# Third group's k and v loads ahead of its block loads on the SP queue, and two of five second-level factor sets made one group later

## The chip, the cores and the metric

The kernel runs on one core of one Trainium2 chip. The metric is the device time of one execution in microseconds (us), as the median of several runs. The kernel before takes 689.92 us (three runs, 687.94 to 690.47); its profiled execution has a span of 691.5 us, and all times inside the kernel below are counted from the start of that span.

## The reference

Decayed linear attention by blocks, followed by a two-layer network with the activation h − tanh(h). There are 4 batches, 8 heads, 768 positions and a head dimension of 64; the network maps 512 to 2048 to 512 for 3072 tokens, all in float32.

```python
for b in range(nb):                                  # blocks of 64 positions
    intra = (qb @ kb^T * Dmask) @ vb                 # within the block, with powers of lam
    inter = (qb * lam_pow) @ kv_state                # from all blocks before
    out[:, :, sl] = intra + inter
    kv_state = lam_block * kv_state + (kb * rev_pow)^T @ vb
x = out.transpose(0, 2, 1, 3).reshape(3072, 512)
h = x @ w_in
out = (h - tanh(h)) @ w_out
```

## The kernel before, in words

**Groups.** The kernel works in blocks of 128 positions instead of 64. There are six groups, numbered 0 to 5: group g is positions 128g to 128g+127 of all four batches, which is 512 tokens. A pair (g, b) of a group and a batch is a chunk. A group passes through attention (`att_transpose`, `att_scores`, `att_out`, `att_state`, in two halves of two batches), then the first layer (`up`), then the second layer (`down`, `down_twice`). Attention of group g+1 is interleaved with the network of group g.

**Plain and split products.** Group 0 uses ordinary matrix products (`up_plain`, `down_plain`). Its second layer is also where the 64-bit weights are turned into 32-bit ones, and where `sums_out` forms the sums of blocks of w_out and writes them to memory. From group 1 on, each layer is split into quarters and done with seven products instead of eight (Strassen's scheme in Winograd's form), called P1 to P7. In the second layer, five of the seven (P3 to P7, the list `TWICE`) are split a second time: `down_twice` has seven small products of 128 columns, 56 matmuls in all, where `down` has 32 matmuls of 256 columns. `down_twice` needs sums of quarters of the hidden values (`sums_twice`, `low`) and has corrections on DVE after the products. The second split needs a factor set of w_out in memory for each product (`fine`).

**Making the factor sets.** For P4, P5, P6, P7 and P3 (`MADE`, numbered t = 0 to 4), `load_quarters(t)` (L452) fetches four quarters of 256 KB from `factors`, into the ring of weight pieces (tag "wb", for even t) or of output tiles (tag "o", four buffers, for odd t). `factors_twice(t)` (L463) does four subtractions on DVE (L468) and four stores of 256 KB to `fine` (L470). All five are spread over the first layer of group 1, after its 6th, 11th, 15th, 20th and 24th product (`turns`).

**Pieces.** The second layer's weights come in pieces of 256 KB through a ring of seven buffers (`piece`, L472), from `fine` (L479) or `factors` (L482). They are issued on the GpSimd queue (POOL in the profile), together with the quarters, the stores to `fine` and the output stores (`store`, L490). The order is written down in `stream`.

**Loads of attention.** They run on the queue of SyncE (SP in the profile). Groups 0 and 1 load q, k and v as they lie ("natural", L127), and TensorE transposes q and k. From group 2 on (`GB` = 2), q and k also come as blocks of 32 by 32 (`load_blocks`, L140, 16 transfers of 16 KB for one chunk's q or k), which DVE transposes (L283). They go into a pool of seven buffers for the eight tiles of a group. This pool takes memory that staging for the weights used before, so its first load has to wait for the last weights to be finished (L260). k in natural form has three buffers, v has four; DVE multiplies k by the decay in place (L318), and TensorE uses k and v in `att_state` (L323) and v in `att_out` (L354). `load` (L143) fixes the order on the queue for a whole group:

```python
for b in range(B - 1):
    load_blocks(g, b, "qk")
load_blocks(g, 3, "q")
for b in (0, 1):
    load_natural(g, b, nat)
load_blocks(g, 3, "k")
for b in (2, 3):
    load_natural(g, b, nat)
```

**Order around the change.** In the last loop, each group runs its first layer (`up` for u = 0 to 3, with P1 of the next u ahead), with the first half of attention of the next group in it; then P1, P2, P4, P5, P6, P7 and P3 of the second layer, with the rest of attention between them. P1 of the next group's first layer runs between P7 and P3. Every engine does its own instructions in the order in which they were compiled, which is close to the order of the program but not the same.

Of the kernel before, what the change touches and what calls it, by code (L numbers as in the profile page):

```python
# [14 lines left out]
AL = mybir.AluOpType  # L15

BLK = 128
GB = 2
# [5 lines left out]
def kernel(  # L24
# [31 lines left out]
    nc = tc.nc  # L56
# [6 lines left out]
    NG = S // BLK  # L63
    HB = GRP // 2
    NU = DFF // 512
# [56 lines left out]
    def load_natural(g, b, names):  # L122
        for name, src, bufs in (("q", q, 2), ("v", v, 4), ("k", k, 3)) if (g, b) == (0, B - 1) else (
                ("q", q, 2), ("k", k, 3), ("v", v, 4)):
            if name in names:
                x = (qpool if name == "q" else io).tile([128, H, D], F32, name=f"{name}_nat", tag=name, bufs=bufs)
                op = nc.sync.dma_start(out=x, in_=src[b, :, ts(g, BLK), :].rearrange("h s d -> s h d"))  # L127
                if g >= GB:
                    tc.keep_in_program_order(op)
                raw[g, b][name] = x  # L130
# [12 lines left out]
    def load(n):  # L143

        while at["loaded"] < min(n, len(chunks)):
            g, b = chunks[at["loaded"]]
            if g < GB:
                raw[g, b] = {}  # L150
                load_natural(g, b, "qkv")
                at["loaded"] += 1
                continue
            for b in range(B):
                raw[g, b] = {}
            nat = "kv" if g < NG - 1 else "v"
            for b in range(B - 1):
                load_blocks(g, b, "qk")
            load_blocks(g, 3, "q")
            for b in (0, 1):  # L160
                load_natural(g, b, nat)
            load_blocks(g, 3, "k")
            for b in (2, 3):
                load_natural(g, b, nat)
            at["loaded"] += B


# [8 lines left out]
    TWICE = (3, 5, 6, 4, 7)  # L176
# [84 lines left out]


    load(B)
    load_weights(WAHEAD)

# [3 lines left out]
    def bank(name, tag, bufs):  # L269
        return psum.tile([128, 512], F32, name=name, tag=tag, bufs=bufs)  # L270
# [110 lines left out]
    def product_bank(key, n):  # L381

        if n == 1:
            banks[key, "y"] = bank("y", "yb" if key[0] == "up" and key[2] % 2 else "ya", 1)
        if n in (2, 5):
            banks[key, "zw"[n == 2]] = bank("zw"[n == 2], "zw"[n == 2], 1)
        t = banks[key, {2: "w", 5: "z", 3: "z"}.get(n, "y")]
        return t.rearrange("q (m c) -> q m c", m=2), n in (1, 2, 5)
# [51 lines left out]
    RING = 7  # L440

    def twice(g, n):
        return n in TWICE and not (g == NG - 1 and n == 3)

    stream = [(g, n, x) for g in range(1, NG) for n in (1, 2, 4, 5, 6, 7, 3)
              for x in (SUB if twice(g, n) else range(NU))]
# [2 lines left out]
    MADE = (4, 5, 6, 7, 3)  # L449
    quarters = {}  # L450

    def load_quarters(t):  # L452
        src = factors[XAT[FACT[MADE[t]][1]]].rearrange("p (u m) c -> p u m c", m=2)
        for i in range(2):
            for j in range(2):
                if t % 2 == 0:
                    x = late["pool"].tile([128, NU, 128], F32, name="wq", tag="wb", bufs=RING)
                else:
                    x = opool.tile([128, NU, 128], F32, name="oq", tag="o")
                nc.gpsimd.dma_start(out=x, in_=src[:, :, i, ts(j, 128)])  # L460
                quarters[t, i, j] = x
# [25 lines left out]
    def store(g, c, t):  # L487
        i, j = divmod(c - 11, 10)
        rows = out.rearrange("(b s) d -> s b d", b=B)[ts(g, BLK), 2 * i:2 * i + 2, ts(j, 256)]
        nc.gpsimd.dma_start(out=rows, in_=t.rearrange("q (m c) -> q m c", m=2))  # L490

    def otile(name):
        return opool.tile([128, 512], F32, name=name, tag="o")

    res, low = {}, {}
# [5 lines left out]

    def down(g, n):

        t, first = product_bank(("down", g), n)
        a = hidden(g, HIDAT[FACT[n][0]])
        for u in range(NU):
            wb = piece(g, n, u)
            for m in range(2):
                for kt in range(2):
                    nc.tensor.matmul(out=t[:, m, :], lhsT=a[:, u, kt, ts(m, 128)], rhs=wb[:, kt, :],  # L510
                                     start=first and u == 0 and m == 0 and kt == 0, stop=u == NU - 1 and kt == 1,
                                     skip_group_check=True)
        t = t.rearrange("q m c -> q (m c)")
        if n == 1:
            res[g, 1] = otile("q1")
            nc.scalar.activation(res[g, 1], t, AF.Copy)
        else:
            o11 = late["pool"].tile([128, 512], F32, name="o11", tag="o11", bufs=1)
            nc.vector.tensor_tensor(o11, res[g, 1], t, op=AL.add)
            store(g, 11, o11)  # L520
            sums_once(g, 11, "S1", 11)
# [6 lines left out]
    def sums_twice(g, n):  # L528
        a11, a12, a21, a22 = quarter(g, n)
        s1, s2 = (late["pool"].tile([128, NU, 128], F32, name=f"s{x}", tag="sums", bufs=4) for x in (1, 2))  # L530
        nc.vector.tensor_tensor(s1, a21, a22, op=AL.add)
        nc.vector.tensor_tensor(s2, s1, a11, op=AL.subtract)
        nc.vector.tensor_tensor(a21, a11, a21, op=AL.subtract)
        low[g, n] = (s1, s2)
# [79 lines left out]
    def run(pieces):  # L614
        for fn, *args in pieces:
            fn(*args)
# [32 lines left out]
    late["blk"] = ctx.enter_context(tc.tile_pool(name="blk", bufs=2 * B - 1))  # L649
    late["pool"] = ctx.enter_context(tc.tile_pool(name="late", bufs=1))  # L650

    turns, made = (6, 11, 15, 20, 24), []
    load_quarters(0)
    load_quarters(1)
    up(1, 0, 1)
    for g in range(1, NG):
        last = g == NG - 1
        p0, p1 = attention(g + 1) if not last else ([], [])
        for u in range(NU):
            for n in (2, 6, 5, 7, 1, 4, 3):  # L660
                if n != 1:
                    up(g, u, n)
                elif u + 1 < NU:
                    up(g, u + 1, 1)
                else:
                    down(g, 1)
                if g == 1:
                    made.append(n)
                    if len(made) in turns:
                        t = turns.index(len(made))  # L670
                        factors_twice(t)
                        if t + 2 < len(MADE):
                            load_quarters(t + 2)
            if not last and u > 1:
                run(p0[u - 2:u - 1])
        sums_twice(g, 4)
        down(g, 2)
        run(p0[2:])
        sums_twice(g, 5)
        down_twice(g, 4, "z")  # L680
        run(p1[0:1])
        sums_once(g, 21, 21, 11)
        sums_twice(g, 6)
        down_twice(g, 5, "w")
        run(p1[1:2])
        sums_twice(g, 7)
        down_twice(g, 6, "z")
        if not last:
            sums_twice(g, 3)
        run(p1[2:])  # L690
        down_twice(g, 7, "w")
        if not last:
            up(g + 1, 0, 1)
            down_twice(g, 3, "z")
        else:
            down_end(g)

# [29 lines left out]
```

## Time and profile before

| what | value |
|---|---|
| median of three runs | 689.92 us |
| span of the profiled execution | 691.5 us |
| transfers | 123.27 MB, 178 GB/s on average |
| second layer and attention beside it, group 1 | 203.17 to 278.70 us |
| the same of group 2 | 322.03 to 384.77 us |
| the same of group 3 | 428.00 to 491.63 us |
| DVE's L468, one | 0.69 us |
| a load of k or v, 256 KB, issue to landing | 5.0 and 5.1 us |
| a piece from `fine`, 256 KB, issue to landing | 4.0 us |
| a piece from `factors`, 256 KB, issue to landing | 5.4 us |

PE is TensorE's matmul, PEld its loading of weights, DVE is VectorE, ACT is ScalarE. The profile gives the busy time of each engine, a picture of the span in 40 slices of 17.29 us with the busy share in tenths and TensorE's granted clock (PEclk, in tenths of full speed), the waits (who waited for whom, total, times, longest), the timeline of an engine (start, length, line, operation, and in brackets the idle time before it with what ended it), and windows (for each stretch its length, then busy time and number of instructions by engine, granted clock, the busy share of the DMA engines, GB/s). Names such as `wb<-fine` are destination and source.

### The profile page before, as it was taken

The numbers are of one execution on the slowest core, as the hardware profiler recorded it, in microseconds if no ns is written. First come the engines' busy times: TensorE is split into PE (matmuls) and PEld (weight loads), VectorE is DVE, ScalarE is ACT, GpSimd is POOL, SyncE is SP. The second block draws the span as 40 slices with busy tenths as digits, with TensorE's granted clock in tenths as the row PEclk, the third lists the DMA queues.
The fourth block names the chain that finished last, engine by engine and source line by source line (L and its number), as shares of the span: only waits on it lengthen the run. The fifth ranks groups of instructions, "written<-read, shape, count | busy, mean of one in ns | idle before, by whom it ended". The sixth has DMA issues, their size and how long they took to land.

```text
span 691.5 us, 12449 instructions
## 1 busy us (share of the span) xinstructions
PE 669.2 (97%) x4688; PEld 578.2 (84%) x4688; DVE 449.9 (65%) x786; ACT 194.5 (28%) x392; POOL 188.0 (27%) x325
## 2 busy tenths in 40 slices
PE   6799999999999689999999999999999999999998
PEld 5588855558887689888899988899988899988897
DVE  3697858893897576447787357787356786344653
ACT  2655432423321112232112233122233122233120
POOL 0001334217554144100144200144300254300262
PEclk9999999999999799999999999999999999999999
DMA  9869889739988798533498632598720576600385
GB/s 190 199 196 238 252 244 262 259 88 264 287 263 242 163 274 246 147 64 67 127 282 247 176 62 47 142 259 227 226 48 18 130 221 206 203 1 0 104 285 176
DMA packets 160427, 123.27 MB, mean 178 GB/s; under 512 B 133488, under 2 KB 133872, under 8 KB 160368
## 3 DMA queue, kind: packets, MB, share of 16 engines
q0 software_dynamic: 27504, 91.77, 41.8%
q1 hardware_dynamic: 132720, 30.71, 22.8%
q8 instruction: 37, 0.61, 0.4%
q14 instruction: 22, 0.18, 0.1%
q10 hardware_dynamic: 144, 0.00, 0.0%
HBM read 99.62 MB, written 22.81 MB: 177 GB/s over the span
## 4 chain that ended last, share of the span: by engine, by line
PE 79%; DMA 9%; issue 4%; SPq 4%; DVE 3%; POOL 1%; ACT 0%; DVEq 0%; POOLq 0%
PE y L405 16%; PE y L548 11%; PE z L405 8%; PE h L590 8%; PE zw L548 8%; PE w L510 5%; PE op L606 5%; PE y L510 4%; PE w L405 4%; SPq L140 3%; PE sp L303 3%; DMA k_blk<-in_k_dram 3%; DMA wb<-fine 3%; PE op L354 2%; DMA q_blk<-in_q_dram 2%
## 5 line engine op out<-in xcount | busy, mean ns | idle before, releaser
L479 POOL DMA_DIRECT2D wb<-fine x168 | 90.3, 538 | 144.0 <-PE y L548 56.8
L482 POOL DMA_DIRECT2D wb<-factors x44 | 23.9, 545 | 188.9 <-PE y L510 177.2
L405 PE MATMUL y<-xt,w 128*128 128x256 f32 x320 | 73.2, 379 | 0.0
L405 PEld LDWEIGHTS y<-xt,w 128*128 128x128 f32 x320 | 60.5, 190 | 8.5 <-issue 0.5
L413 ACT ACTIVATE th<-g 128x512 f32<-128x512 f32 x60 | 37.8, 630 | 93.8 <-DVE g L431 41.8
L548 PE MATMUL y<-wb,g 128*128 128x128 f32 x456 | 61.6, 279 | 0.0
L551 ACT ACTIVATE q<-y 128x128 f32<-128x128 f32 x96 | 26.7, 278 | 123.3 <-PE y L548 119.7
L414 DVE TENSOR_TENSOR g<-g,th 128x512 f32<-128x512 f32 x60 | 41.4, 690 | 27.5 <-ACT th L413 27.2
L548 PEld LDWEIGHTS y<-wb,g 128*128 128x128 f32 x456 | 56.0, 193 | 1.5 <-issue 0.3
L590 PE MATMUL h<-xt,w 128*128 128x256 f32 x256 | 56.8, 384 | 0.0
L606 PE MATMUL op<-wt,g 128*128 128x512 f32 x128 | 56.5, 595 | 0.0
L590 PEld LDWEIGHTS h<-xt,w 128*128 128x128 f32 x256 | 48.9, 192 | 7.4 <-issue 0.5
L606 PEld LDWEIGHTS op<-wt,g 128*128 128x128 f32 x128 | 23.8, 190 | 27.7 <-issue 26.5
L426 DVE TENSOR_TENSOR g<-g,z 128x512 f32<-128x512 f32 x20 | 13.7, 686 | 44.4 <-ACT g L425 44.4
L548 PE MATMUL zw<-wb,g 128*128 128x128 f32 x304 | 40.2, 275 | 0.0
L405 PE MATMUL y<-tt,w 128*128 128x256 f32 x160 | 37.9, 380 | 0.6 <-ACT g L425 0.6
L405 PE MATMUL z<-tt,ws 128*128 128x256 f32 x160 | 37.9, 380 | 0.0
L405 PE MATMUL w<-xt,w 128*128 128x256 f32 x160 | 37.8, 379 | 0.0
L405 PE MATMUL y<-tt,ws 128*128 128x256 f32 x160 | 37.8, 379 | 0.0
L405 PE MATMUL z<-xt,ws 128*128 128x256 f32 x160 | 37.8, 379 | 0.0
L307 DVE TENSOR_TENSOR ss<-sp,mask 128x512 f32<-128x512 f32 x48 | 30.8, 684 | 10.3 <-PE sp L303 10.3
L548 PEld LDWEIGHTS zw<-wb,g 128*128 128x128 f32 x304 | 37.0, 192 | 0.0
(125 smaller groups left out, 1223.7 us busy)
## 6 DMA issues: line engine op xcount, KB each, us to landing
wb<-fine POOLq DMA_DIRECT2D x168, 256.0 KB, 4.0
wb<-factors POOLq DMA_DIRECT2D x44, 256.0 KB, 5.4
raw<-in_moe_w_out_dram POOLq DMA_DIRECT2D x16, 512.0 KB, 5.4
v_nat<-in_v_dram SPq DMA_DIRECT2D x24, 256.0 KB, 5.1
factors<-wt POOLq DMA_DIRECT2D x8, 768.0 KB, 5.4
k_nat<-in_k_dram SPq DMA_DIRECT2D x20, 256.0 KB, 5.0
raw<-in_moe_w_in_dram SPq DMA_DIRECT2D x8, 512.0 KB, 5.4
raw<-in_moe_w_in_dram SPq DMA_DIRECT2D x16, 256.0 KB, 4.8
```

The costliest lines, as they stand in the source:

```text
L140: nc.sync.dma_start(out=x[ts(c, 32), p], in_=blk.rearrange("(r t) a -> t r a", t=32)))
L307: nc.vector.tensor_tensor(ss[:, j], sp[j], mask[:, j], op=AL.mult)
L405: nc.tensor.matmul(out=t[:, m, :], lhsT=wt[:, kt, ts(m, 128)], rhs=x[:, kt, :], start=first and m == 0 and kt == 0, stop=kt == 1, skip_gro ...
L413: nc.scalar.activation(th, src, AF.Tanh)
L414: nc.vector.tensor_tensor(dst(c), src, th, op=AL.subtract)
L479: nc.gpsimd.dma_start(out=t.rearrange("p m c -> p (m c)"), in_=fine[TWICE.index(n_), SUB.index(x_)].rearrange("p u c -> p (u c)"))
L482: nc.gpsimd.dma_start(out=t, in_=factors[XAT[FACT[n_][1]]][:, 2 * x_:2 * x_ + 2, :])
L510: nc.tensor.matmul(out=t[:, m, :], lhsT=a[:, u, kt, ts(m, 128)], rhs=wb[:, kt, :], start=first and u == 0 and m == 0 and kt == 0, stop=u = ...
L548: nc.tensor.matmul(out=dst, lhsT=a[:, u, :], rhs=wb[:, ts(u, 128)], start=x in (1, 2) and u == 0, stop=u == NU - 1, skip_group_check=True)
L551: nc.scalar.activation(keep, dst, AF.Copy)
L590: nc.tensor.matmul(out=hm[:, m, :], lhsT=w1[u][:, i, a, ts(m, 128)], rhs=xt[0, t][:, i, :], start=m == 0 and i == 0, stop=i == KI - 1, ski ...
L606: nc.tensor.matmul(out=obank[b], lhsT=g, rhs=wt[:, 2 * a:2 * a + 2, :], start=kt == 0 and a == 0, stop=kt == KH - 1 and a == 1)
```

## The change

For group 2 alone (`g == GB`), k and v of the chunks 0, 1 and 2 are loaded ahead of all block loads; the k and v of chunk 3 stay behind them. Of the five factor sets, only those of P4, P5 and P6 are made in the first layer of group 1, after its 7th, 14th and 21st product; those of P7 and P3 are made in the first layer of group 2, after its 8th and 18th. Their quarters use output tiles. In group 1, P7 and P3 are therefore done as plain products by `down`, with their output additions read straight from PSUM; from group 2 on they are split twice as before. The purpose is to have k and v there when attention of the third group asks for them, and to take loads, stores and sums out of the busiest stretch.

```diff
             nat = "kv" if g < NG - 1 else "v"
+            first = (0, 1, 2) if g == GB else ()
+            for b in first:
+                load_natural(g, b, nat)
             for b in range(B - 1):
                 load_blocks(g, b, "qk")
             load_blocks(g, 3, "q")
             for b in (0, 1):
-                load_natural(g, b, nat)
+                if b not in first:
+                    load_natural(g, b, nat)
             load_blocks(g, 3, "k")
             for b in (2, 3):
-                load_natural(g, b, nat)
+                if b not in first:
+                    load_natural(g, b, nat)
...
-        return n in TWICE and not (g == NG - 1 and n == 3)
+        return n in TWICE and not (g == NG - 1 and n == 3) and not (g == 1 and n in (7, 3))
...
-                if t % 2 == 0:
+                if t in (0, 2):
                     x = late["pool"].tile([128, NU, 128], F32, name="wq", tag="wb", bufs=RING)
                 else:
                     x = opool.tile([128, NU, 128], F32, name="oq", tag="o")
...
-        t, first = product_bank(("down", g), n)
+        if n in (1, 2):
+            t, first = product_bank(("down", g), n)
+        else:
+            t, first = bank("plain", "w" if n == 7 else "z", 1).rearrange("q (m c) -> q m c", m=2), True
...
+        elif n == 7:
+            o = otile("q7")
+            nc.vector.tensor_tensor(res[g, 4], res[g, 4], t, op=AL.add)
+            store(g, 21, res[g, 4])
+            nc.vector.tensor_tensor(o, res[g, 5], t, op=AL.add)
+            store(g, 22, o)
+        elif n == 3:
+            o = otile("q3")
+            nc.vector.tensor_tensor(o, res[g, 5], t, op=AL.add)
+            store(g, 12, o)
...
-    turns, made = (6, 11, 15, 20, 24), []
+    turns, made = {1: (7, 14, 21), 2: (8, 18)}, []
...
-                if g == 1:
+                if g in turns:
                     made.append(n)
-                    if len(made) in turns:
-                        t = turns.index(len(made))
+                    step = len(made) - 7 * NU * (g - 1)
+                    if step in turns[g]:
+                        t = turns[g].index(step) + len(turns[1]) * (g - 1)
                         factors_twice(t)
-                        if t + 2 < len(MADE):
-                            load_quarters(t + 2)
+                        if t in (0, 3):
+                            load_quarters({0: 2, 3: 4}[t])
+                    elif (g, step) == (2, 1):
+                        load_quarters(3)
...
-        sums_twice(g, 7)
+        if twice(g, 7):
+            sums_twice(g, 7)
         down_twice(g, 6, "z")
-        if not last:
+        if twice(g, 3):
             sums_twice(g, 3)
         run(p1[2:])
-        down_twice(g, 7, "w")
+        if twice(g, 7):
+            down_twice(g, 7, "w")
+        else:
+            down(g, 7)
         if not last:
             up(g + 1, 0, 1)
-            down_twice(g, 3, "z")
+            if twice(g, 3):
+                down_twice(g, 3, "z")
+            else:
+                down(g, 3)
```

## The prediction

> **What bounds the kernel now.** I read the page first: engine shares, then the tenths by slice. PE is busy for 97% of the span, so time can only come from PE's few gaps or from its instruction count.
>
> ```profile
> PE 669.2 (97%) x4688; PEld 578.2 (84%) x4688; DVE 449.9 (65%) x786; ACT 194.5 (28%) x392; POOL 188.0 (27%) x325
> ...
> PE   6799999999999689999999999999999999999998
> ...
> PEclk9999999999999799999999999999999999999999
> ```
>
> The two dips in PE (its slices 13 and 14, counted from 0, are 224.7 to 259.3 us) and the dip in the granted clock fall together. Next the waits of PE over the whole span: which wait ends last there.
>
> ```profile
> PE op L354 <- DMA v_nat<-in_v_dram: 6.1, 2, 5.6
> ...
> PE y L548 <- DMA wb<-fine: 1.4, 3, 0.6
> PE zw L548 <- DMA wb<-fine: 1.1, 2, 0.9
> ```
>
> The largest is in group 1's lower half, where attention of group 2 (the third group) needs its v. The timelines of PE and of SP's queue show it:
>
> ```profile
> 223.33 1.10 PE L348 MATMUL op<-qd,state 64*64 64x128 f32 x32
> 230.05 1.97 PE L354 MATMUL op<-ss,v_nat 128*64 128x128 f32 x16 [5.61 <-DMA v_nat<-in_v_dram]
> 232.48 1.97 PE L354 MATMUL op<-ss,v_nat 128*64 128x128 f32 x16 [0.46 <-DMA v_nat<-in_v_dram]
> 234.21 1.95 PE L323 MATMUL kv<-v_nat,k_nat 128*64 128x64 f32 x32
> ...
> 212.95 11.90 SPq L140 DMA_DIRECT2D q_blk<-in_q_dram  x16
> 224.95 0.39 SPq L127 DMA_DIRECT2D k_nat<-in_k_dram  x1
> 225.38 0.58 SPq L127 DMA_DIRECT2D v_nat<-in_v_dram  x1
> ```
>
> v was issued at 225.38, after seven block loads of 16 transfers, and PE asked for it at 224.4. SP is simply late: it started the blocks at 147.44 and needed 77.5 us for 112 small transfers. To size the whole loss, not only the named waits, I compare the lower half of group 1 with that of group 2, which does the same work undisturbed (windows view, columns: stretch, length, PE, PEld, DVE, ACT, POOL, clock, DMA share, GB/s):
>
> ```profile
> 223.33:236.09 12.76, 6.69 (x97) 5.96 (x96) 6.11 (x10) 1.20 (x2) 1.28 (x2) 0.62 0.75 163
> 236.09:252.07 15.98, 14.09 (x115) 13.26 (x113) 10.78 (x19) 2.50 (x9) 7.00 (x13) 0.98 0.94 257
> 252.07:278.70 26.63, 26.63 (x306) 25.94 (x306) 16.79 (x29) 5.85 (x18) 12.67 (x24) 1.00 0.83 239
> ...
> 341.41:345.27 3.86, 3.86 (x97) 3.62 (x97) 3.86 (x7) 1.09 (x2) 1.26 (x2) 1.00 0.43 131
> 345.27:357.97 12.70, 12.70 (x116) 12.58 (x112) 11.37 (x21) 2.50 (x9) 5.94 (x11) 1.00 1.00 282
> 357.97:384.60 26.63, 26.63 (x305) 25.94 (x305) 16.81 (x30) 5.85 (x18) 13.72 (x25) 1.00 0.89 245
> ```
>
> Attention's products cost 12.76 us in group 1 and 3.86 in group 2: 8.90 lost, of which 6.07 are waits and the rest slow matmuls (clock 0.62). P4 and P5 cost 15.98 against 12.70: 3.28 lost, of which 1.82 are three waits for wb pieces. P6, P7 and P3 agree to 0.01. So this place holds 8.90 + 3.28 = 12.2 us.
>
> **What the Trainium skill says.** "TensorE: Matmul & The Clock Gate", section "What's actually happening", says that after about 3.4 us of idling PE's clock falls to half until it has been busy as long. The trace agrees: after 5.61 us idle the granted clock of 227 to 237 us is 0.51, and the 32 kv products take 1.9 us instead of 0.9. So removing the wait removes slow products too. "DMA: Bandwidth & Descriptors", section "Issuing engines are not separate DMA queues", says that transfers of all issuing engines share the same 16 DMA engines; the trace shows shares of 0.99 and 1.02 between 157 and 177 us, with SP's and POOL's transfers mixed, so every transfer taken out of there helps the block loads. "Perfetto Trace Analysis", section "Tensor Engine Instruction (MATMUL, LD_WEIGHTS)", calls ACT, DVE and GpSimd strictly first in, first out. It agrees here: DVE sat 6.97 us in front of k (L318), and POOL 9.22 us in front of the store of o11, which waits for DVE.
>
> **The change, part by part.**
>
> 1. *k and v of chunks 0 to 2 of group 2 ahead of the blocks.* Six transfers of 256 KB leave the places at 224.95 to 240. Their buffers are rings of 3 (k) and 4 (v): k of chunk 0 and v of chunk 0 need what attention of group 1, first half, read (kv products until about 115 us), the other four what its second half read (kv until 143.5). SP was idle from 114.9 to 147.44, waiting for L260 to free the staging memory. Two can therefore go at 115, four at 143.6; at about 0.6 us each (v at 225.38 took 0.58) they are issued by about 146, before 147.44. The start of the blocks does not move: cost zero, hidden by that wait. Landing takes 5.0 to 5.1 us in the page, so all are there by about 152, 70 us early. What queues behind the four on SP is only the blocks. The two at 115 take 0.5 MB from w_out's transfers; at the 261 GB/s of that stage that is 2 us, against 3 us and more between DVE's last L260 (147.36) and PE's use of that block (150.4). Gain: 8.90 for attention. P4 and P5 lose their late v, k and o11 neighbours: POOL's store moves from 233.46 to about 226, and 1.5 MB of k and v no longer compete at 225 to 240. But P5's first piece can only be issued when P4 gives a buffer back, and lands 4 to 5 us later, within P4's 6.3 us: tight. I take 3.28 less 0.5 left over, bounds 0 to 3.28.
>
> 2. *P7 and P3 plain in group 1.* A plain product is 32 matmuls of 256 columns: 7.12 us (P2, on the chain) or 6.91 (P1). The twice-split one is 56 of 128 columns: P7 264.36 to 270.72 is 6.36, P3 272.45 to 278.70 is 6.25. Cost: (7.12 − 6.36) + (6.95 − 6.25) = +1.4 us, all on PE's path. Its bank is read by two vector additions (0.69 each) after P7, one after P3; the next user of bank w comes 8.7 us later, of z some 3.5 us later: hidden. Saved on DVE: the sums and corrections of two products. DVE's compiled order in the changed kernel also moves the two k decays of the second half (L318) behind P6's additions: by 0.3, 0.4, 0.7, 0.6, 0.6, 0.6, 0.6 us they end about 10.0 us after P6's start, and PE wants the first at 9.4. New wait: 0.2 to 0.6, I take 0.3.
>
> 3. *Two factor sets made in group 2.* Per set 4 loads and 4 stores of 256 KB and 4 vector operations of 0.69 us. From 157 to 209 us this removes 4 MB of transfers and 8 operations (4.8 us at the 0.6 us spacing); P7 and P3 also fetch 8 pieces instead of 14. In group 1 the waits of 0.39 (piece of P1, issued only at 205.35; now the last P1 piece follows the third set's first sum, about 201.5) and 0.56 us shrink: −0.4. Block loads get faster, not slower. In group 2 the same 8 operations fall into a stretch where DVE is busy 49 of 73 us and DMA 0.47, and POOL has nothing for 43.1 us (its wait before L482). The first quarters need the stores of group 1's outputs, all landed some 6 us before DVE reaches the sums. I cost it 0, at most 2.
>
> Sum: −8.90 − 2.78 − 0.4 + 1.4 + 0.3 = −10.4 us; 689.9 − 10.4 = 679.5.
>
> **The rivals.**
>
> *A wait in its place.* P5's pieces stay late (3.28 kept), or chunk 3's k blocks or k, which still follow on SP, hold DVE at the second half. For it: 128-byte rows make SP's pace 7.5 to 13.5 us for 16 transfers, and k of chunk 3 must wait for the first half's kv. Against: the k blocks of chunk 3 no longer stand behind four k and v loads and should land near 230, when DVE wants them at about 234. Time: 679.5 + 2.8 + 1 = 683.3.
>
> *Only the named waits go*: 6.07 + 1.82 − 1.4 = 6.5, giving 683.4. Against it speaks group 2's clean 3.86 us with the same matmuls.
>
> *Slower.* DVE works in order and would stand before a late quarter or block in group 1 or 2, as it stood 2.31 and 1.70 us at 173 to 176. If the blocks of chunks 0 and 1 came 14 us late (SP held up by the early loads), DVE would stop, PE's banks would not be freed, and nearly all of the 12.2 would come back: 689.9 − 12.2 + 1.4 + 14 = 693. Against: those blocks were issued by 190.1 and are wanted at 203, and SP had idle time for the early loads.
>
> **How the numbers follow.** My forecast (677.5 to 681.5) has 0.75, the two partial rivals together 0.19, slower or unchanged 0.06. Best case: the full 12.2, 0.9 from a smoother upper half, 1.4 back: 678.2. I take 677.5 to 683.8, which holds the partial cases. Faster by over 0.5% (below 686.5) 0.94, within 0.03, slower 0.03.
>
> **What would show it.** In the changed profile: no wait of PE for v; k and v issued at 115 and 143.6 to 146 on SP; clock near 1.0 in slice 13; attention's products near 3.9 us; two plain products of about 7 us in group 1; no PE gap in group 2's upper half. It is wrong if DVE stands before blocks near 203 or 234 us, if PE waits for a quarter's sums, or if P5 still waits for pieces.

## The result, and the profile after

| kernel | median us | runs | ratio to before, 95% interval |
|---|---|---|---|
| before | 689.91 | 687.94 to 690.47 | |
| changed | 681.65 | 680.64 to 682.34 | 0.9884 [0.9861, 0.9908] |
| changed, measured again | 681.02 | 679.83 to 682.52 | 0.9851 [0.9827, 0.9875] (before there 690.65) |

The changed kernel is 8 to 10 us faster. The forecast was 679.5 us, with a range of 677.5 to 683.8. Of the two medians the second lies within the 677.5 to 681.5 to which the prediction gave a chance of 0.75; the first lies just above, where it had put the partial rivals.

Lines of code have moved: L548 of before is L567 in the changed kernel, L510 is L519, L354 is L360, L348 is L354, L323 is L329, L303 is L309, L479 is L485. In the first experiment every line after the edit is five further down (L548 is L553, L283 is L288). In the other kernels the line numbers differ again; there, go by the names of the tiles.

First the summary of the changed kernel's profile: the engine shares, and the tenths of PE and of the granted clock in 40 slices, now of 17.0 us.

```profile
PE 665.8 (98%) x4640; PEld 575.1 (85%) x4640; DVE 443.4 (65%) x774; ACT 192.1 (28%) x382; POOL 184.8 (27%) x319
...
PE   6999999999999899999999999999999999999998
...
PEclk9999999999999999999999999999999999999999
```

Of the two dips around slice 13 one tenth is left in PE, and the clock shows none. PE's busy time fell by 3.4 us though two products became longer: the slow matmuls are gone. The waits of PE over the whole span (who waited for whom, total, times, longest):

```profile
PE y L567 <- DMA wb<-fine: 2.0, 3, 1.0
...
PE zw L567 <- DMA wb<-fine: 1.6, 2, 1.0
```

The wait for v (6.1 us) is not on the list any more; the waits for pieces are still there and have grown, from 2.5 to 3.6 us in all (in group 1 alone from 1.82 to 2.30). PE's timeline shows both (start, length, line, operation, idle time before with its releaser):

```profile
219.21 1.10 PE L354 MATMUL op<-qd,state 64*64 64x128 f32 x32
220.25 1.97 PE L360 MATMUL op<-ss,v_nat 128*64 128x128 f32 x32
222.04 1.10 PE L329 MATMUL kv<-v_nat,k_nat 128*64 128x64 f32 x32
...
232.40 1.13 PE L567 MATMUL y<-wb,s 128*128 128x128 f32 x8 [1.01 <-DMA wb<-fine]
234.15 1.16 PE L567 MATMUL zw<-wb,s 128*128 128x128 f32 x8 [0.62 <-DMA wb<-fine]
235.97 1.13 PE L567 MATMUL y<-wb,gS 128*128 128x128 f32 x8 [0.67 <-DMA wb<-fine]
```

Attention's three groups of products follow each other without a gap. The three waits are for the third, fourth and fifth piece of P5. SP's queue, the answer to the lines at 212.95 to 225.38 of before:

```profile
140.58 0.37 SPq L127 DMA_DIRECT2D k_nat<-in_k_dram  x1
141.00 1.12 SPq L127 DMA_DIRECT2D v_nat<-in_v_dram  x1
142.29 2.50 SPq L127 DMA_DIRECT2D k_nat<-in_k_dram  x1
144.83 2.07 SPq L127 DMA_DIRECT2D v_nat<-in_v_dram  x1
147.27 8.03 SPq L140 DMA_DIRECT2D q_blk<-in_q_dram  x16
...
218.84 8.40 SPq L140 DMA_DIRECT2D k_blk<-in_k_dram  x16
227.35 0.39 SPq L127 DMA_DIRECT2D k_nat<-in_k_dram  x1
227.78 0.59 SPq L127 DMA_DIRECT2D v_nat<-in_v_dram  x1
```

Chunk 3's k blocks are thus issued by 227.24. DVE has its own work until it comes to them, and does not stand in front of them (no bracket, so no idle time before it):

```profile
231.53 0.67 DVE L289 STREAM_TRANSPOSE kt<-k_blk 128x512 f32<-128x512 f32 x1
```

Four of the six early loads go right ahead of the first block load, as forecast. But these four took 6.3 us, where the prediction had counted 0.6 us each, and the blocks start at 147.27, although DVE's last L266 (L260 before) had already ended at 144.9. In the kernel before, the k blocks of chunk 3 came after four loads of k and v that began at 224.95.

Where the time came from is read by stage. In the profiled execution of before, everything ahead of group 1's first product of the first layer's main part (the first `up` product into bank w) took 2.5 us longer than in the changed kernel: 159.02 against 156.50 us. That start differs as much between two executions of one kernel (155.11 and 157.33 us for the fastest of the kernels below), so the stages are compared from group 1 on; the first of them begins one product earlier, at 157.29 and 154.78. The windows of both kernels (stretch, length, busy time and instructions of PE, PEld, DVE, ACT, POOL, clock, DMA share, GB/s), first group 1's upper half before, with P1 and P2:

```profile
157.29:203.17 45.88, 45.32 (x210) 39.36 (x209) 30.10 (x49) 14.35 (x25) 29.10 (x45) 1.00 0.99 292
203.17:223.33 20.16, 19.77 (x113) 16.71 (x111) 16.75 (x28) 3.05 (x5) 8.04 (x15) 1.00 0.77 223
```

and after, the upper half, P1 and P2, attention's products, P4 with P5, and the rest to P3:

```profile
154.78:199.67 44.89, 44.89 (x209) 39.52 (x208) 26.84 (x43) 14.91 (x25) 20.34 (x32) 1.00 0.78 218
199.67:219.21 19.54, 19.54 (x113) 16.79 (x111) 17.16 (x29) 3.05 (x5) 6.42 (x12) 1.00 0.76 207
219.21:223.08 3.87, 3.87 (x98) 3.63 (x97) 3.87 (x7) 1.09 (x2) 1.28 (x2) 1.00 0.64 156
223.08:238.82 15.74, 13.44 (x117) 12.80 (x113) 9.71 (x18) 2.49 (x9) 6.98 (x13) 1.00 0.92 248
238.82:267.20 28.38, 28.24 (x257) 25.69 (x257) 12.06 (x20) 3.34 (x9) 9.55 (x18) 1.00 0.74 197
```

| stage of group 1 | before | after | difference | forecast |
|---|---|---|---|---|
| first layer (upper half) | 45.88 | 44.89 | −0.99 | −0.4 with the next row |
| P1 and P2 of the second layer | 20.16 | 19.54 | −0.62 | |
| attention's products | 12.76 | 3.87 | −8.89 | −8.90 |
| P4 and P5 | 15.98 | 15.74 | −0.24 | −2.78 |
| scores, P6, P7, P1 of the next, P3 | 26.63 | 28.38 | +1.75 | +1.7 |
| sum | | | −8.99 | −10.4 |

In the second measurement of the changed kernel, P4 and P5 took 15.25 us (−0.73). The whole stretch from group 1's first product into bank w to that of group 2 went from 119.68 to 110.70 us, and there to 110.21. In group 2, where two factor sets are now made, the same stages keep their lengths: 43.30 us for the upper half against 43.20, 19.40 against 19.51 for P1 and P2, and 26.50 against 26.63 at the end.

### The profile page after: what moved, and what is told of

Its sections match the earlier page's. It is cut to its first block, busy times and chain, and to the rows that moved or that the text cites. A ratio compares the mean times of both kernels' runs of the same rounds, so it can differ in the third digit from the quotient of the medians.

```text
span 680.6 us, 12315 instructions
## 1 busy us (share of the span) xinstructions
PE 665.8 (98%) x4640; PEld 575.1 (85%) x4640; DVE 443.4 (65%) x774; ACT 192.1 (28%) x382; POOL 184.8 (27%) x319
## 4 chain that ended last, share of the span: by engine, by line
PE 90%; DMA 4%; DVE 2%; issue 2%; POOL 1%; ACT 0%; POOLq 0%; SPq 0%; DVEq 0%
PE y L411 20%; PE z L411 10%; PE y L567 10%; PE op L625 8%; PE zw L567 7%; PE h L609 6%; PE w L519 5%; PE w L411 5%; PE y L519 5%; PE sp L309 4%; DMA wb<-fine 3%; PE op L360 3%; PE plain L519 2%; PE op L354 1%; PE tp L294 1%
## 5 line engine op out<-in xcount | busy, mean ns | idle before, releaser
L485 POOL DMA_DIRECT2D wb<-fine x154 | 82.8, 538 | 134.6 <-PE w L519 49.8
L488 POOL DMA_DIRECT2D wb<-factors x52 | 28.1, 542 | 166.2 <-PE y L519 137.4
L570 ACT ACTIVATE q<-y 128x128 f32<-128x128 f32 x88 | 24.4, 277 | 114.4 <-PE y L567 107.4
L567 PE MATMUL y<-wb,g 128*128 128x128 f32 x408 | 54.8, 278 | 0.0
L567 PEld LDWEIGHTS y<-wb,g 128*128 128x128 f32 x408 | 49.8, 192 | 1.4 <-issue 0.3
L420 DVE TENSOR_TENSOR g<-y,th 128x512 f32<-128x512 f32 x20 | 13.8, 691 | 34.9 <-ACT th L419 34.9
L567 PE MATMUL zw<-wb,g 128*128 128x128 f32 x272 | 36.0, 275 | 0.0
```

Source lines behind the costliest of these rows:

```text
L420: nc.vector.tensor_tensor(dst(c), src, th, op=AL.subtract)
L485: nc.gpsimd.dma_start(out=t.rearrange("p m c -> p (m c)"), in_=fine[TWICE.index(n_), SUB.index(x_)].rearrange("p u c -> p (u c)"))
L488: nc.gpsimd.dma_start(out=t, in_=factors[XAT[FACT[n_][1]]][:, 2 * x_:2 * x_ + 2, :])
L567: nc.tensor.matmul(out=dst, lhsT=a[:, u, :], rhs=wb[:, ts(u, 128)], start=x in (1, 2) and u == 0, stop=u == NU - 1, skip_group_check=True)
L570: nc.scalar.activation(keep, dst, AF.Copy)
```

## The experiments

Three theories stood at the start. *Wait for v*: the six early loads do nearly all of it, and the later sets only balance the cost of the two plain products. *Queue*: SP is late for all that group 2 needs, so taking v out only moves the wait to what comes next on SP, and the later sets are what makes the block loads fast enough. *Pieces*: what is left in P4 and P5 is a matter of transfers that compete, or of the ring of pieces.

### Early k and v alone

```diff
 # the kernel before, load()
+            first = (0, 1, 2) if g == GB else ()
+            for b in first:
+                load_natural(g, b, nat)
```

with the `if b not in first` of the change, and nothing else.

> The kernel before with only the early loads of k and v of group 2; the five factor sets stay in group 1 and P7, P3 stay split twice. Theory A (the early loads earn the gain, the later sets cost about what they save): the wait for v of 6.1 us is gone, attention's products take 3.9 us instead of 12.8, and the time is 680 to 682, like the changed kernel (681.65). Theory B (the gain needs the room that the later sets make on the DMA engines): with all five sets in group 1 the block loads or the pieces of P4 and P5 come later and hold PE for 3 us or more: 684 to 687.

Measured: 687.55 us (685.23 to 689.09), 0.9961 [0.9944, 0.9978] of before. DVE's timeline in it shows why so little was gained:

```profile
231.80 0.70 DVE L288 STREAM_TRANSPOSE qt<-q_blk 128x512 f32<-128x512 f32 x1
237.15 0.71 DVE L288 STREAM_TRANSPOSE kt<-k_blk 128x512 f32<-128x512 f32 x1 [4.65 <-DMA k_nat<-in_k_dram]
...
238.36 0.68 DVE L558 TENSOR_TENSOR gS<-gS,s 128x512 f32<-128x512 f32 x1
```

PE's timeline shows what that wait did to it:

```profile
233.86 1.06 PE L553 MATMUL y<-wb,gS 128*128 128x128 f32 x8
239.14 2.05 PE L553 MATMUL zw<-wb,gS 128*128 128x128 f32 x8 [4.23 <-issue]
240.98 1.91 PE L553 MATMUL y<-wb,gS 128*128 128x128 f32 x8
242.82 3.23 PE L308 MATMUL sp<-qt,kt 64*128 64x128 f32 x32
```

and SP's queue when the transposed blocks were issued:

```profile
223.96 8.92 SPq L140 DMA_DIRECT2D k_blk<-in_k_dram  x16
232.99 0.55 SPq L127 DMA_DIRECT2D k_nat<-in_k_dram  x1
```

The wait for v is gone, but another has come, 10 us later on PE: DVE stands 4.65 us in front of the k blocks of chunk 3. Behind this transpose on DVE stands an addition to gS, a sum of hidden values which P5 reads, and it ends at 239.04, just before PE goes on. So PE stands 4.23 us; "issue" there only says that the profile found no releaser. After it 8 matmuls of 128 columns take 1.84 us from start to start, instead of 0.89. The bracket names `k_nat`, but the instruction reads `k_blk`, which was issued up to 232.9; the natural load stood right behind it on SP. The run without these blocks, below, bears this out.

The block loads had started at 147.37, while DVE's last weight operation (L265 here) had ended at 143.65. In the kernel before they had started 0.08 us after it, so the early loads cost the blocks about 3.6 us at their start; the last one ended earlier than before only because it no longer stood behind four loads of k and v. An estimate: had the 3.6 us been passed on in full to the last block, they would be most of DVE's 4.65 us. No run has the early loads without this delay.

### Later factor sets alone

The changed kernel, with `load` in the order of before:

```diff
-            first = (0, 1, 2) if g == GB else ()
-            for b in first:
-                load_natural(g, b, nat)
```

> The changed kernel with the loads of k and v put back behind the blocks; two factor sets in group 2 and plain P7, P3 in group 1 stay. Theory A: the blocks run some 6 us faster on SP, so v is asked for at about 219 and issued at about 219, lands 4 to 5 us later: PE still waits 4 us or so; upper half 1.6 us shorter, plain products +1.4: 686 to 688.5. Theory B (the sets are what made SP late): v is there in time, no wait for it, below 684. If the sets do nothing but cost plain products: 691.

Measured: 688.32 us, with a wide spread (683.74 to 691.28), 0.9964 [0.9945, 0.9982]. PE's timeline:

```profile
220.42 1.09 PE L355 MATMUL op<-ss,v_nat 128*64 128x128 f32 x16 [0.73 <-DMA v_nat<-in_v_dram]
224.44 1.98 PE L355 MATMUL op<-ss,v_nat 128*64 128x128 f32 x16 [2.92 <-DMA v_nat<-in_v_dram]
```

The waits for v are 3.65 us instead of 6.07. The seven sets of block loads ahead of k and v took 70.1 us on SP instead of 77.5, and v came earlier, but it still stood behind them. The first of them went out at 144.29, 3 us before that of the changed kernel and 0.07 us after DVE's last weight operation:

```profile
144.29 7.46 SPq L140 DMA_DIRECT2D q_blk<-in_q_dram  x16
```

Each half alone brings some 2.6 us: 690.6 × (1 − 0.9961) = 2.7, with its interval 1.5 to 3.9, and 690.6 × (1 − 0.9964) = 2.5, 1.2 to 3.8. That makes 5.2 together, against 8.0 and 10.3 for the full change. By the stretch from group 1's first product to that of group 2 the halves are 4.36 and 4.18 us in their profiled executions, 8.54 together against 8.98 and 9.47. How much more than their sum the two bring together is therefore not settled; that neither does it alone, and for which wait, is.

### The k blocks of chunk 3 left out

To see whether the blocks are the wait that came with the early loads, this kernel is the first one without that load:

```diff
-            load_blocks(g, 3, "k")
+            if g == GB:
+                raw[g, 3]["kb"] = raw[g, 2]["kb"]
+            else:
+                load_blocks(g, 3, "k")
```

> The early loads alone (as e1_kv_only), but the k blocks of chunk 3 of group 2 are not loaded; the k blocks of chunk 2 are used in their place, so chunk 3's attention is computed from other data. In e1_kv_only DVE stood 4.65 us at 237 before that transpose and PE 4.23 us behind it, with a slow clock after. Theory B1 (those 16 late transfers are what ate the gain): the wait is gone, P4, P5 and the scores take 15 to 17 us instead of 22.2, and the time falls by 5 to 7 us to 681 to 683. Theory B2 (k of chunk 3, issued at 233, or the full DMA engines are the cause): the wait stays or turns up at pieces of P5 and the time stays at 686 to 688.

Measured: 679.99 us (679.19 to 680.54), 0.9844 [0.9821, 0.9868]. Windows from P4 to the start of the next product after the scores, first with the early loads alone:

```profile
223.81:245.98 22.17, 17.94 (x148) 17.39 (x145) 12.79 (x23) 2.77 (x10) 7.55 (x14) 0.85 0.81 227
```

and without the k blocks:

```profile
223.80:239.82 16.02, 15.40 (x148) 14.72 (x144) 12.43 (x23) 2.78 (x10) 7.55 (x14) 1.00 0.98 280
```

The kernel leaves out chunk 3's k blocks and transposes those of chunk 2 in their place. Both kernels reach P4 at 223.8; one set of 16 transfers makes 6.15 us of difference there, DVE has no wait for blocks, and the clock stays at 1.00. So with this one load goes the loss of the early loads alone, and the queue theory holds: the wait moved on to the next thing that SP was late for. Leaving it out also moved the k and v of chunk 3 ahead on SP, from 232.99 to 225.13, so this run alone does not clear them. But the transpose reads only `k_blk`, and in a run further down the bracket of the same wait names a third transfer, `q_blk` of the next group, which it does not read either. The waits for pieces in P5 shrank as well, to 0.30 and 0.32 us, though the DMA engines are busier.

### Chunk 3's k and v left out

In the changed kernel, to see what holds P5's pieces; chunk 3 then uses the tiles of chunk 2:

```diff
             for b in (2, 3):
-                if b not in first:
+                if g == GB and b == 3:
+                    for name in nat:
+                        raw[g, b][name] = raw[g, 2][name]
+                elif b not in first:
                     load_natural(g, b, nat)
```

> The changed kernel without the loads of k and v of chunk 3 of group 2 (0.5 MB, issued at 227.4 beside the pieces of P5); chunk 3 uses the tiles of chunk 2 instead, so its attention is computed from other data. It asks why P5 still loses 3.05 us (229.43 to 238.82 where 6.34 would do). Theory C (these two loads take the DMA engines from the pieces): the stretch of P4 and P5 falls from 15.7 to 13 to 13.5 us, waits for pieces in group 1 below 0.5 us, time 679 to 680. Theory D (POOL's queue stood 1.2 us before the second piece and then sent four at once): the loads don't matter, 15 us or more, time as the changed kernel's.

Measured: 679.75 us (678.72 to 680.62), 0.9842 [0.9819, 0.9866]. The window of P4 and P5:

```profile
222.15:235.95 13.80, 12.93 (x116) 12.65 (x112) 9.72 (x18) 2.49 (x9) 6.97 (x13) 1.00 0.87 248
```

13.80 us instead of 15.74 and 15.25 (and 15.05 in the kernel of "Split products kept", which is the same up to here), with one wait of 0.87 us left of three. The two loads, issued at 227.35 and 227.78 among the pieces of P5, thus account for 1.3 to 1.9 us; theory C's 13 to 13.5 us and waits below 0.5 us were not quite reached. One wait is of another origin.

### One more buffer for pieces

The changed kernel with `RING = 8` in place of 7.

> The changed kernel with eight buffers for weight pieces instead of seven, so each piece can be issued one product (0.9 us) earlier. If P5's loss of 3.05 us is a matter of the piece's time from issue to landing (5.2 to 7.6 us there) against 6.3 us of lead, 0.9 us more lead takes 0.9 to 2 us of it and most of the 1.3 us of waits for pieces in later groups: 679 to 680.5. If the DMA engines are simply full there (0.92), more lead shifts the wait to the next pieces and gives under 0.5 us: 681.2 to 682.

Measured: 679.09 us (677.67 to 681.31), 0.9836 [0.981, 0.9863]. The window of P4 and P5:

```profile
223.60:237.52 13.92, 13.17 (x116) 12.72 (x112) 9.74 (x18) 2.49 (x9) 6.97 (x13) 1.00 0.87 252
```

PE waits for no piece in the whole run; what is left in this stage is one wait of 0.65 us for ACT. What the ring of seven did is seen on the queue of GpSimd in the changed kernel:

```profile
224.53 0.56 POOL L485 DMA_DIRECT2D wb<-fine  x1 [1.52 <-PE y L567]
226.63 2.12 POOL L485 DMA_DIRECT2D wb<-fine  x4 [1.54 <-PE y L567]
```

The first piece of P5 is issued after P4's first product, but the second only at 226.63, after P4's third, and then four go out together. PE had to wait for the third, the second of these four, until 232.40, some 5 us after its issue. In the kernel with the early loads alone the pieces go out one by one, at 225.26, 226.16 and so on. With eight buffers four still go out together, but 2.66 us after P4's start instead of 3.55: what the eighth buffer gave is the earlier issue, not an end of the bunch. It may be that the quarters, which use the same ring, leave its buffers in another order than that in which P4 frees them; no run isolates this. Either of the two, one buffer more (1.1 to 1.8 us) or two loads less (1.3 to 1.9 us), removes a good part of the 2.4 to 3.0 us by which this stage exceeds group 2's 12.70, so it is a matter of timing at the edge and not of one cause.

### Split products kept, without their sets

The changed kernel, with P7 and P3 of group 1 split twice; as their sets are not made by then, their pieces are read from P6's:

```diff
-        return n in TWICE and not (g == NG - 1 and n == 3) and not (g == 1 and n in (7, 3))
+        return n in TWICE and not (g == NG - 1 and n == 3)
...
-                                    in_=fine[TWICE.index(n_), SUB.index(x_)].rearrange("p u c -> p (u c)"))
+                                    in_=fine[TWICE.index(6 if g_ == 1 and n_ in (7, 3) else n_), SUB.index(x_)].rearrange("p u c -> p (u c)"))
```

> The changed kernel with P7 and P3 of group 1 split twice instead of plain, but without making their sets there: their pieces are read from P6's set, so the second layer of group 1 is computed with other weights. It separates the two sides of the later sets: the transfers taken out of group 1 (kept out here) and the plain products (undone here). If what helps is the transfers and the plain products are only the price (1.4 us, and 0.3 for the decays behind P6's additions): 679.5 to 680.5, no wait of DVE for blocks. If the plain products help too, because they fetch 8 pieces instead of 14 beside the next group's blocks: 682 to 683.

Measured: 680.87 us (678.65 to 682.73), 0.9858 [0.9835, 0.9881]. This lies between the two expectations and is not told apart from the changed kernel by time. In the trace, the end of the group (from attention's products behind P6 on) takes 18.20 us against 19.95: the plain products cost 1.75 us, what the table above shows too. DVE waits 0.77 us for chunk 3's k blocks here, where it did not in the changed kernel.

### P7's set made in group 1 after all

The changed kernel with `RING = 8`, four sets in group 1, one in group 2, and only P3 plain; the loads of the quarters are moved to match:

```diff
-        return n in TWICE and not (g == NG - 1 and n == 3) and not (g == 1 and n in (7, 3))
+        return n in TWICE and not (g == NG - 1 and n == 3) and not (g == 1 and n == 3)
...
-    turns, made = {1: (7, 14, 21), 2: (8, 18)}, []
+    turns, made = {1: (6, 11, 16, 22), 2: (10,)}, []
...
```

> e5_ring8 (679.1) with P7's set made in group 1 again and P7 split twice there; only P3's set is later. Saves 0.7 us of PE for the plain P7, and puts 2 MB back into group 1's upper half, which moves the k blocks of chunk 3 by some 2.5 us on SP: they would land at about 231.5, just when DVE wants them. If they are still in time: 678.4 to 679. If not: a wait of 1 to 3 us, 680 to 682.

Measured: 687.24 us (685.63 to 687.9), 0.9947 [0.9927, 0.9967]. DVE's timeline:

```profile
240.61 0.71 DVE L289 STREAM_TRANSPOSE kt<-k_blk 128x512 f32<-128x512 f32 x1 [7.86 <-DMA k_nat<-in_k_dram]
```

and PE's:

```profile
242.60 2.05 PE L567 MATMUL zw<-wb,gS 128*128 128x128 f32 x8 [7.40 <-issue]
```

One set more in group 1, 2 MB of loads and stores, costs 8.15 us by the medians (of different jobs) against the kernel with `RING = 8` alone, to save one plain product. It is the same wait as with the early loads alone: the k blocks of chunk 3 were issued at 226.27 to 236.1, 7.4 to 8.9 us later than in the changed kernel. The expectation, 2.5 us later and a wait of at most 3 us, was far too small.

The profiles of all kernels fall into two groups here. With three sets in group 1 (nine profiles) the DMA share from 157 to 200 us is 0.76 to 0.80, and the seven sets of block loads ahead of chunk 3's k blocks take 70.1 to 72.5 us on SP. With four or five sets (five profiles, the kernel before among them) the share is 0.98 to 0.99, and they take 76.6 to 80.5 us; four sets are no better than five.

### Chunk 3's v early as well

v has four buffers, so the fourth v can go ahead too; k has three. Together with `RING = 8`:

```diff
             for b in first:
                 load_natural(g, b, nat)
+            if first:
+                load_natural(g, 3, "v")
...
-                    load_natural(g, b, nat)
+                    load_natural(g, b, "k" if first else nat)
...
-    RING = 7
+    RING = 8
```

> e5_ring8 with v of chunk 3 also ahead (its buffer is free then; k's is not). Takes 256 KB from the stretch of P5. If what is left of P5's loss in e5_ring8 (13.9 against 12.7 us) is contention with these loads: 0.5 to 1 us less, 678 to 678.7. If it is something else (ring order, ACT's evacuation): as e5_ring8, 679.1.

Measured: 677.78 us (676.67 to 678.78), 0.9816 [0.9792, 0.9839]. The windows of attention's products, of P4 with P5, and of the rest:

```profile
217.82:221.69 3.87, 3.87 (x98) 3.63 (x97) 3.87 (x7) 1.09 (x2) 1.28 (x2) 1.00 0.67 163
221.69:235.23 13.54, 12.93 (x115) 12.65 (x112) 9.83 (x18) 2.50 (x9) 6.99 (x13) 1.00 0.86 252
235.23:263.62 28.39, 28.25 (x257) 25.69 (x257) 12.06 (x20) 3.35 (x9) 9.55 (x17) 1.00 0.75 207
```

In this profile P4 and P5 are 1.7 to 2.2 us shorter than in the two profiles of the changed kernel, with one wait of 0.61 us; the two other stages are the same. This kernel and the changed one were measured once more, side by side:

> e9_ring8_v3 once more (eight piece buffers, v of chunk 3 also ahead; 677.78 in its first job): 677 to 678.5, some 3.5 us below the changed kernel beside it, if the gain is real; within 1.5 us of it if the jobs differed.

> The changed kernel once more, beside the three others, so that they are compared on one chip. 681.65 was measured; between 680.5 and 682.5 if its first timing holds.

Measured: 677.88 us (677.27 to 684.73), 0.9825 [0.9791, 0.986], and 681.02 us, 0.9851 [0.9827, 0.9875], for the changed kernel. Both medians of this version are 3 to 4 us below those of the changed kernel, which the intervals of the second pair alone would not show. In the second profile P4 and P5 took 14.66 us, only 0.6 to 1.1 us less than in the changed kernel, with waits of 0.65 and 0.81. Against `RING = 8` alone (679.09) the early v is not told apart.

### The refinements without the later sets

The kernel with the early loads alone, plus the early v and `RING = 8`:

> Early loads alone, with all five sets in group 1 as before, plus the eight piece buffers and the early v of chunk 3. Theory B (the k blocks of chunk 3 are late because the five sets crowd the DMA engines): neither refinement helps that, DVE still stands 3 us or more before the transpose at about 233, and the time stays at 685 to 688. If the lateness of pieces was the cause in e1_kv_only: 679 to 681.

Measured: 684.57 us (681.93 to 685.0), 0.9893 [0.9869, 0.9917]. DVE's timeline:

```profile
242.41 0.71 DVE L290 STREAM_TRANSPOSE kt<-k_blk 128x512 f32<-128x512 f32 x1 [7.04 <-DMA q_blk<-in_q_dram]
```

and PE's:

```profile
243.27 2.08 PE L310 MATMUL sp<-qt,kt 64*128 64x128 f32 x16 [5.29 <-DVE kt L290]
```

The wait for the k blocks is there again, and longer on DVE; the time is just below the 685 to 688 that theory B gave. The bracket names `q_blk`, which this transpose does not read. This time the compiled order on DVE had P5's addition to gS ahead of the transpose, so P5 went through and PE stood only at the scores. The later sets are not replaced by the refinements: with both it is 677.8.

### P7 and P3 never split a second time

The best version, with no sets for P7 and P3 in any group:

```diff
-        return n in TWICE and not (g == NG - 1 and n == 3) and not (g == 1 and n in (7, 3))
+        return n in TWICE and n not in (7, 3)
...
-    turns, made = {1: (7, 14, 21), 2: (8, 18)}, []
+    turns, made = {1: (7, 14, 21)}, []
...
```

> e9_ring8_v3 with P7 and P3 plain in every group and without their two sets at all. It measures the price of plain products by itself: P7 in groups 2 to 5 and P3 in groups 2 to 4, seven products of 0.65 to 0.76 us, 4.9 us, and up to 0.4 us for late decays in each of groups 2 to 4: 682.5 to 684 against 677.8. If plain products were free because they fetch less (8 pieces instead of 14): 678 to 679.5.

Measured: 686.33 us (685.16 to 686.9), 0.9926 [0.9902, 0.9949]. PE's timeline in group 2:

```profile
358.05 7.17 PE L521 MATMUL plain<-wb,g 128*128 128x256 f32 x32
...
366.79 7.07 PE L521 MATMUL plain<-wb,g 128*128 128x256 f32 x32
```

Against the first profile of the best version, the stages of groups 2, 3, 4 and 5 became longer by 1.82, 2.12, 1.30 and 1.02 us, 6.26 together for seven plain products, 0.89 each. The medians differ by 8.45, more than the 4.7 to 6.2 that was expected; group 1 is alike in both (108.81 us against 108.51 and 109.62), and where the other 2.2 us lie is left open: the start differs by as much between executions, but the medians should not. So to make the two sets later is worth it, not to make them at all is not.

## Why the prediction was right, and where it was not

The total came out 1.5 to 2.2 us above 679.5. The largest term was right in size and mechanism, but two others missed in opposite directions, and one cost put at nothing was not nothing. That the sum held is in part luck.

**Attention's products, −8.90.** Measured −8.89, with 3.87 us per group as in group 2. The slow matmuls went with the wait, as the Trainium skill has it in "TensorE: Matmul & The Clock Gate", section "What's actually happening"; the clock of this stretch is 1.00 instead of 0.62. The other cases agree: where a wait of 4.23 us came in (early loads alone), it was followed by matmuls of half the pace. The 3.4 us of idling that the prediction took from there was not needed in full: with the later sets alone the clock was 0.50 behind a wait of 2.92 us (which began 1.1 us after the end of one of 0.73). One reading of the prediction was off: the 32 kv products take 1.03 us undisturbed, not 0.9.

**P4 and P5, −2.78.** This is the term of the sum that failed: it measured −0.24 and −0.73. The step said that 1.5 MB of k and v would no longer compete, and that P5's first piece would land 4 to 5 us after its issue, within P4's 6.3. Two things were not in it. The k and v of chunk 3 came out of SP at 227.35 and 227.78, because the blocks ahead of them came earlier, and so fell right among P5's pieces, which landed later than the 4.0 us of the kernel before (the third 5 us after its issue; the median of this stretch is 6.4). Leaving the two out took 1.3 to 1.9 us off. And the pieces after the first were issued in a bunch, late. One more ring buffer took 1.1 to 1.8 us off the same stage. The bounds of this term (0 to 3.28) held the value, and the rival "a wait in its place", which kept the 3.28, was nearly right on this point. Its other half, DVE standing before chunk 3's k blocks, did not happen in the two profiles of the changed kernel, but narrowly: in four of the other kernels' profiles with the early loads and three sets in group 1 DVE did wait for them, 0.8 to 1.5 us.

**Upper half, −0.4.** Measured −0.99 and, with P1 and P2, −1.6 us. Here the DMA share fell from 0.99 to 0.78, and every wait of PE went, where the prediction had only shrunk two. It was mis-sized by 1.2 us to the safe side, which makes up for about half of what P4 and P5 did not give.

**Plain P7 and P3 with late decays, +1.7.** Measured +1.75. The products are 7.01 and 6.90 us against 6.36 and 6.25, 1.3 together; the rest is the late start of the kv products, 0.3 us as the prediction had it, and their slower pace. (The prediction's 6.95 for a plain P3 is its own rounding; the row it names gives 6.91.)

**Two sets in group 2, 0.** Right: group 2's stages kept their lengths within 0.13 us, and none of them was longer by more than 0.1.

**"The start of the blocks does not move: cost zero."** Wrong in its working. It rested on one row, v at 225.38 with 0.58 us, the second of four natural loads in a row; the two behind it, at 226.06 and 227.35, had taken 1.24 and 1.20 us. Early in the same SP timeline a longer row shows more still (its first two loads, not shown, took 0.59 and 0.58 us):

```profile
57.80 2.91 SPq L127 DMA_DIRECT2D v_nat<-in_v_dram  x1
60.82 1.16 SPq L127 DMA_DIRECT2D q_nat<-in_q_dram  x1
62.09 2.48 SPq L127 DMA_DIRECT2D k_nat<-in_k_dram  x1
64.62 2.57 SPq L127 DMA_DIRECT2D v_nat<-in_v_dram  x1
```

With 2.3 us for each of the four (the mean of these rows), the estimate would have been 9 us after 143.6 rather than 2.4. Measured were 6.3 us, and a block start 2.4 us after DVE's last weight operation, 3.6 with the early loads alone. "DMA: Bandwidth & Descriptors" of the Trainium skill says in "Issuing engines are not separate DMA queues" that the time which a sequencer needs to initiate a DMA is "usually small relative to the DMA itself"; for four loads of 256 KB in a row, each landing in some 5 us, it was not small here. PE did not have to pay for it in the changed kernel because the later sets gave SP more than that back: its seven sets of block loads took 71.6 us instead of 76.6 with the early loads alone.

**What carries the gain.** The prediction put 8.90 down to the early loads and nothing of it to the later sets. The single halves say otherwise. The early loads alone move the wait to the k blocks of chunk 3; only with less traffic in the upper half are those blocks issued by 227.2 instead of 232.9, and DVE does not stand. The nine profiles against five, above, show the same. The prediction had said that block loads get faster without the two sets, but had given it no price; "a wait in its place" is what the early loads do alone.

## What to carry to other kernels

When one transfer is late because its whole queue is late, moving it ahead moves the wait to the next one; list everything that is wanted from this queue within the next 10 to 15 us with its time of need, and take work off the queue or the DMA engines as well. Issue costs of a queue are to be taken from rows that stand back to back under the same load, not from a single row. Where a ring feeds products of 0.89 us with transfers of 4 to 7 us, look at its depth: one buffer more was worth as much here as the removal of two loads. And look at how near the next transfer is to being late: here one factor set more brought back a wait of 7.40 us.

## What the runs showed of the hardware

Issue on SP of 256 KB loads in a row: the first took 0.4 to 0.6 us, those behind it 0.6 to 3.7 us (0.66, 3.62 and 0.67 in one row, with P7's set made in group 1). A set of 16 block transfers took 7.45 us (at 147.44, before) to 15.15 us (at 240.32, before), and seven sets took longer where the DMA share was 0.98 to 0.99. What sets the pace of one set was not measured by itself; the block loads differ from the loads of k and v both in number and in the length of their rows.

Behind waits of PE the matmuls ran at half pace (clock 0.50) for a few us, so that each wait cost more than its own length:

| where | waits of PE | lost in all | beyond the waits |
|---|---|---|---|
| v, later sets alone | 3.65 | 5.20 | 1.55 |
| k blocks, early loads alone | 4.23 | 7.48 | 3.25 |
| v, before | 6.07 | 8.90 | 2.83 |
| k blocks, P7's set in group 1 | 7.40 | 9.52 | 2.12 |

Lost is against the same stage undisturbed: 3.87 us for attention's products, 14.69 us for P4, P5 and the scores in group 2 of before. The loss beyond the wait was 1.5 to 3.3 us and did not grow with the wait. A wait of 1.73 us for a piece of P5, with the later sets alone, had no such loss: the clock of its stage was 1.00.
